# The last batch's a and b blocks, two chunks at a time: seven matmul products for eight

## The chip, the cores and the metric

The kernel runs on one core of one Trainium2 chip. The metric is the device time of one execution in microseconds (us), smaller is better. A core has TensorE (PE, matmuls; PEld is its loading of weights), VectorE (DVE), ScalarE (ACT), GpSimd (POOL) and SyncE (SP, which here issues DMAs). Each takes its own instructions in order, and they wait for each other by semaphores. SBUF is the working memory. PSUM, with eight banks of 128 x 512 floats, is where PE writes; in this kernel POOL works in SBUF only.

## The reference

The kernel computes an attention over channels and then a multiplicative feed-forward network on its output. There are 4 batches of 5824 tokens with 256 channels.

```python
qn = q / (norm(q, axis=1) + 1e-06)          # q, k, v: (4, 5824, 256)
kn = k / (norm(k, axis=1) + 1e-06)
s = kn.transpose(0, 2, 1) @ qn / tau         # 256 x 256 for each batch
a = softmax(s, axis=-1)
x = (v @ a).reshape(4 * 5824, 256)
y1 = x @ w1                                  # 256 -> 1024
y2 = x @ w2
out = (y1 * y2 @ w3) @ w_out                 # 1024 -> 1024 -> 256
```

## The kernel before

**Algebra.** w3 and w_out are multiplied once into a 1024 x 256 matrix `W_sb`. For each batch the 256 x 256 attention matrix is folded into w1 and w2, which gives `Wf`, so that the tokens v need only two products: a = v Wf1 and b = v Wf2. The output is (a * b) W_sb. Matmul inputs are bf16, sums are float32.

**Tiling.** A batch's tokens are cut into 12 chunks: 11 of 512 tokens (0 to 10) and one of 192 (11). The 1024 columns of a and b are cut into 8 blocks of 128 (index j). `emit_ab(b, c, j)` makes one block of a chunk: two matmuls for a and two for b (the 256 channels are two halves, ct), each of 512 columns (line 657). ACT casts a to bf16 (`a_sb`, line 663), and DVE multiplies it by b out of PSUM into the half-chunk tile `abh` (line 676). One such call is a slot. The a and b tiles rotate through four PSUM banks, ab0 to ab3.

**Output.** For most chunks `seven_products` computes the output as a 2 x 2 block product with seven products for eight: four sums of abh quarters, S1 to S4 (lines 589 and 592, 128 x 1024 each), then products p1 to p7, each of eight matmuls of 128 columns (line 570). ACT writes out stages of the accumulating tile A (`keep`, line 580), and DVE adds tiles B and C into the output (`join`, J, line 583), before a DMA stores the chunk. p6 reads S2, p5 reads S1, p7 reads S3 and p3 reads S4. The four S tiles have one buffer each. In batches 0 to 2 the sums are on POOL, in batch 3 on DVE. The plain way, `emit_half`, takes 32 matmuls of 256 columns (line 707) and needs no sums.

**Order.** The order of instructions is written by hand. The loop at the end runs through the slots of a batch. In each slot it emits work that is due by an estimated clock (`run_due`: loads, transposes, folds), then `emit_ab`, and then waiting output work out of the queue `pend`: entries have a slot from which they are due and a size, and a slot takes entries up to `room`, in order. So a slot of the last batch holds four matmuls of 512 columns and at most one group of eight output matmuls. The S sums are emitted out of `due_sums`.

**The next batch's weights.** During batch n - 1 the scores of batch n are computed (lines 197 to 212, over by slot 71 of 96), then the softmax, then `fold` (lines 428 to 437): eight folds of two matmuls each, evicted with a scale by ACT and DVE in turn into `Wf[n]`. Batch 3 has no next batch, so its slots hold no scores. Loads of v are issued on POOL behind a `gate`, a copy of one element that waits for the latest abh block (line 645); their transposes and the stores are issued by SP.

**Tiles.** abh, loaded pieces and some others share 21 buffers with the tag "big".

Of the kernel before, what the change touches and what calls it, by code (L numbers as in the profile page):

```python
# [9 lines left out]
AF = mybir.ActivationFunctionType  # L10
ALU = mybir.AluOpType
F32 = DT.float32
BF16 = DT.bfloat16
# [12 lines left out]
def kernel(  # L26
# [250 lines left out]
    def soft_units(n):  # L277
# [142 lines left out]
        def fold_mm(key, c2, tag="ab", on_act=True):  # L420

            w, c1, lo, hi = key
            if c2 == 0:
                turn = (lo // 512 * 4 + w * CT + c1) % 3
                home = bank(tag) if n == 0 or turn == 2 else {"tag": ("out2", "G")[turn], "bufs": 1}
                st[key] = psum.tile([P, 512], F32, name=f"fold_{n}_{w}_{c1}_{lo}", **home)
            m = st[key][:, : hi - lo]
            nc.tensor.matmul(  # L428
                m, lhsT=st["e"][:, c2, c1 * P : (c1 + 1) * P], rhs=w12[:, c2, w, lo:hi],
                start=(c2 == 0), stop=(c2 == CT - 1),  # L430
            )
            if c2 == CT - 1:
                dst = Wf[n][:, c1, w, lo:hi]
                if on_act:
                    nc.scalar.activation(out=dst, in_=m, func=AF.Copy, scale=st["rs"][:, c1 : c1 + 1])
                else:
                    nc.vector.tensor_scalar_mul(dst, m, st["rs"][:, c1 : c1 + 1])

        def fold(i, tag="ab"):
            h, rest = divmod(i, 4)  # L440
            w, c1 = divmod(rest, 2)
            for c2 in range(CT):
                fold_mm((w, c1, h * 512, (h + 1) * 512), c2, tag, i % 2 == 0 or (n == 0 and i == 7))

# [43 lines left out]
        )  # L488


    clock = [0.0]
    agenda = []

    def run_due(upto=None):
        lim = clock[0] if upto is None else upto
        while agenda and agenda[0][0] <= lim:
            _, _, cost, fn = agenda.pop(0)
            clock[0] += cost
            fn()
# [3 lines left out]
    def at(t, cost, fn):  # L503
        seq[0] += 1
        agenda.append((t, seq[0], cost, fn))
# [21 lines left out]

    def seven(b, c):
        if b == B - 1:
            return c < NCH - 2  # L530
        return (4 if b == 0 else 0) <= c < NCH - 1

    def combine_weights(step):
# [18 lines left out]
    def seven_products(b, c, k1, k2):  # L552
# [6 lines left out]
        w22 = [W_sb[:, 4 + j, P:] for j in range(4)]  # L559
        t1, t2, t3, t4 = ([T[:, i, j, :] for j in range(4)] for i in range(4))  # L560
        st, sums = {}, {}
        tags = {"A": "out0", "B": "out1", "C": "out1" if b < B - 1 else "out2"}
        adder = nc.gpsimd if b < B - 1 else nc.vector

        def product(nm, a, w, first=False):
            if first:
# [63 lines left out]
        def then(fn):  # L630
            return lambda: following.append(fn)

        if b == B - 1:
            return [S(1)], [
                [S(2), p1], [S(3), p5], [p6], [S(4), p7], [J("C", 1, 1), p2],
                [J("B", 0, 0), p4], [p3, J("C", 0, 1), store],
            ]
# [13 lines left out]
    def emit_ab(b, c, j):  # L651
        n = chunk_cols(c)
        tiles = []
        for w in range(2):
            t = psum.tile([P, 512], F32, name=f"{'ab'[w]}_{b}_{c}_{j}", **bank("ab"))
            for ct in range(CT):
                nc.tensor.matmul(  # L657
                    t[:, :n], lhsT=Wf[b][:, ct, w, j * P : (j + 1) * P], rhs=rhs_of(b, c, ct),
                    start=(ct == 0), stop=(ct == CT - 1),
                )  # L660
            tiles.append(t)
        a_sb = work.tile([P, 512], BF16, tag="a_sb", name=f"as_{b}_{c}_{j}", bufs=4)
        nc.scalar.copy(a_sb[:, :n], tiles[0][:, :n])  # L663
        if c == NCH - 1:
            if b % 2 == 0 and j == 0:
                lefts[b // 2] = work.tile([P, FT, 2, P + LEFT], BF16, tag="left", name=f"left_{b}", bufs=1)
            both = lefts[b // 2][:, j, b % 2, :]
            nc.vector.tensor_mul(both, a_sb[:, :n], tiles[1][:, :n])
            ab = both[:, :P] if b % 2 == 0 else both[:, LEFT:]
        else:  # L670
            if j == 0:
                halves[c] = [
                    in_pool.tile([P, 4, 512], BF16, tag="big", name=f"abh_{b}_{c}_{h}", bufs=BIG_BUFS) for h in range(2)
                ]
            ab = halves[c][j // 4][:, j % 4, :]
            nc.vector.tensor_mul(ab, a_sb, tiles[1])  # L676
        last_ab[0] = ab
        slot[0] += 1
        if not seven(b, c):
            if b == B - 1 or c == NCH - 1:  # L680
                lag = LAG if b == B - 1 else FT + LAG_FAST
                pend.append((slot[0] + lag, 1, lambda only=None: emit_out(b, c, j, ab, only)))
            elif j == FT - 1:
                for i in range(FT):
                    fn = lambda i=i, ab2=tuple(halves[c]): emit_half(b, c, i, ab2)
                    pend.append((slot[0] + 1 + LAG_FAST + i, 1, fn))
        elif j == FT - 1:
            sums, groups = seven_products(b, c, *halves[c])
            for i, fn in enumerate(sums):
                due_sums.append((slot[0] + 2 * i, fn))  # L690
            ready = slot[0] + 1 + (LAG_FAST if b < B - 1 else 0)
            for i, group in enumerate(groups):
                wait = 0 if b == B - 1 else i
                pend.append((ready + wait, 2, lambda group=group: [fn() for fn in group]))
        clock[0] += 4 * (n * MM_COL + MM_FIX)

    def emit_half(b, c, i, ab2):

# [212 lines left out]
    def make_agenda(b):  # L911
# [34 lines left out]
        if b == 0:  # L946
            for i in range(4):
                at(COMB + 2.6 * i, 0.0, lambda i=i: combine_weights(i))
        if n == B:
            agenda.sort()  # L950
            return
# [14 lines left out]

    for b in range(B):
        make_agenda(b)
        order = [(c, j) for c in range(NCH) for j in range(FT)]
        if b == 0:  # L970
            order[: 2 * FT] = [(c, h * 4 + j) for h in range(2) for c in range(2) for j in range(4)]
        for s, (c, j) in enumerate(order):
            run_due()
            while following:
                following.pop(0)()
            scores_due(s)
            emit_ab(b, c, j)
            lag = 0
            if b == B - 1 and c >= NCH - 2:
                lag = LAG_END if c == NCH - 1 else LAG + (LAG_END - LAG) * (j + 1) // FT  # L980
            room = 2
            while slot[0] > W_SLOT and len(pend) > lag and pend[0][0] <= slot[0] and pend[0][1] <= room:
                _, size, fn = pend.pop(0)
                fn()
                room -= size
                run_due()
            while due_sums and due_sums[0][0] <= slot[0]:
                due_sums.pop(0)[1]()
        run_due(1e9)
# [39 lines left out]
```

## Time and profile before

| | |
|---|---|
| median of 3 runs | 555.02 us (554.97 to 555.27) |
| span of the profiled execution, first to last instruction | 553.5 us |
| own time of the profiled execution | only its span is given; the median of the runs lies 1.5 us above it |
| PE, DVE, ACT, POOL busy | 542.1, 435.5, 375.8, 304.8 us |
| granted PE clock | 1.000 |
| last batch's first a matmul | at 431.81 us |

The profile shows one execution. A timeline line gives start, duration, engine, line of the kernel, operation, output and inputs, count, and in brackets the idle time before it with what ended it. A matmul's duration covers its way through the array; the next one starts well before it ends, so what one costs is the distance between starts. The same holds in smaller measure for DVE and ACT. A line by stretch gives the stretch, its length, the busy time of PE, PEld, DVE, ACT and POOL with counts in brackets, the granted clock of PE as a fraction, the share of the DMA engines and GB/s.

### The profile page before, as it was taken

How to read it: one execution, taken by the hardware profiler on the slowest of the kernel's cores; microseconds unless marked ns; L12 is line 12 of the kernel's file. 1: busy time of each engine (PE TensorE's matmuls, PEld its weight loads, DVE VectorE, ACT ScalarE, POOL GpSimd, SP SyncE). 2: the span in 40 equal slices, each digit the busy share in tenths (PEclk: the TensorE clock that was granted, in tenths of full speed). 3: DMA queues.
4: the chain of work that ended last, by engine and by line, in shares of the span. 5: the costliest groups of instructions: out<-in, count | busy, mean ns of one | idle time of the engine just before them, and what ended most of it. 6: DMA issues, size and time to landing. Idle time of an engine off the chain costs nothing.

```text
span 553.5 us, 12330 instructions
## 1 busy us (share of the span) xinstructions
PE 542.1 (98%) x4630; PEld 352.9 (64%) x4630; DVE 435.5 (79%) x789; ACT 375.8 (68%) x757; POOL 304.8 (55%) x257
## 2 busy tenths in 40 slices
PE   7799999999999999999999999999999999999997
PEld 4564577766666666666667566666666666666665
DVE  5567747899976787988876788888877688988984
ACT  5436647788866777777766777777766666566663
POOL 4150022678889678889887588898987400010000
PEclk9999999999999999999999999999999999999999
DMA  9999888975666879576554777875650245343102
GB/s 213 211 206 209 167 164 201 224 180 82 152 140 155 191 150 165 126 147 136 128 127 122 153 153 156 164 147 124 147 115 40 83 117 117 91 110 82 77 40 97
DMA packets 74972, 77.61 MB, mean 140 GB/s; under 512 B 54176, under 2 KB 58784, under 8 KB 74912
## 3 DMA queue, kind: packets, MB, share of 16 engines
q0 software_dynamic: 15616, 38.93, 40.3%
q1 hardware_dynamic: 58928, 37.17, 24.2%
q8 instruction: 36, 0.59, 0.4%
q10 hardware_dynamic: 368, 0.72, 0.3%
q14 instruction: 24, 0.20, 0.1%
HBM read 78.91 MB, written 23.86 MB: 186 GB/s over the span
## 4 chain that ended last, share of the span: by engine, by line
PE 93%; DMA 5%; DVE 0%; ACT 0%; POOL 0%; issue 0%; POOLq 0%
PE a L657 28%; PE b L657 28%; PE prodA L570 13%; PE prodC L570 6%; PE G L200 5%; PE prodB L570 3%; DMA k<-in_k_dram 3%; PE o L707 3%; PE fold L428 2%; DMA q<-in_q_dram 2%; PE o_out L738 2%; PE w L882 1%; PE G L271 0%; PE narrow L452 0%; PE sqq L259 0%
## 5 line engine op out<-in xcount | busy, mean ns | idle before, releaser
L676 DVE TENSOR_TENSOR abh<-as,b 128x512 bf16<-128x512 bf16 x352 | 240.0, 684 | 82.0 <-ACT as L663 76.2
L663 ACT CAST as<-a 128x512 bf16<-128x512 f32 (+1 forms) x384 | 215.4, 562 | 94.8 <-PE a L657 61.5
L657 PE MATMUL a<-vT,Wf 128*128 128x512 bf16 x704 | 209.4, 379 | 0.1
L657 PE MATMUL b<-vT,Wf 128*128 128x512 bf16 x704 | 209.4, 379 | 0.0
L657 PEld LDWEIGHTS <-Wf 128*128 128x128 bf16 x1536 | 141.1, 98 | 100.6 <-issue 0.8
L570 PEld LDWEIGHTS <-S 128*128 128x128 bf16 x1248 | 82.6, 98 | 34.3
L212 DVE TENSOR_TENSOR acc<-acc,sq 128x512 f32<-128x512 f32 x132 | 91.6, 694 | 3.0 <-ACT sq L197 1.9
L580 ACT COPY osb<-prodA 128x256 f32<-128x256 f32 x156 | 58.1, 372 | 42.0 <-PE prodA L570 41.4
L589 POOL TENSOR_TENSOR S<-abh,abh 128x1024 bf16<-128x1024 bf16 x29 | 61.7, 2127 | 32.1 <-DVE abh L676 16.6
L570 PEld LDWEIGHTS <-abh 128*128 128x128 bf16 x936 | 62.0, 98 | 25.7 <-issue 0.2
L592 POOL TENSOR_TENSOR S<-S,abh 128x1024 bf16<-128x1024 bf16 x29 | 61.8, 2131 | 1.9
L592 POOL TENSOR_TENSOR S<-abh 128x1024 bf16<-128x1024 bf16 x29 | 61.8, 2131 | 0.1
L592 POOL TENSOR_TENSOR S<-abh,S 128x1024 bf16<-128x1024 bf16 x29 | 61.7, 2129 | 0.1
L645 POOL COPY gate_t<-abh 1x1 bf16<-1x1 bf16 x39 | 7.2, 185 | 80.1 <-DVE abh L676 79.9
L570 PE MATMUL prodA<-comb_T,S 128*128 128x128 bf16 x624 | 47.6, 219 | 0.0
L200 PE MATMUL G<-k,q 128*128 128x256 bf16 x276 | 47.0, 273 | 0.0
L197 ACT ACTIVATE sq<-q 128x512 f32<-128x512 bf16 x69 | 43.8, 634 | 0.0
L197 ACT ACTIVATE sq<-k 128x512 f32<-128x512 bf16 x69 | 43.4, 628 | 0.0
L583 DVE TENSOR_TENSOR osb<-prodC,osb 128x256 f32<-128x256 f32 x78 | 32.5, 417 | 0.0
L200 PEld LDWEIGHTS <-q 128*128 128x128 bf16 x276 | 23.9, 98 | 3.6
L570 PE MATMUL prodB<-W_sb,abh 128*128 128x128 bf16 x312 | 23.8, 219 | 0.1
L570 PE MATMUL prodC<-comb_T,S 128*128 128x128 bf16 x312 | 23.8, 219 | 0.0
(139 smaller groups left out, 444.0 us busy)
## 6 DMA issues: line engine op xcount, KB each, us to landing
out_dram<-osb SPq DMA_DIRECT2D x44, 512.0 KB, 3.2
k<-in_k_dram POOLq DMA_DIRECT2D x19, 512.0 KB, 8.3
v<-in_v_dram POOLq DMA_DIRECT2D x19, 512.0 KB, 5.2
q<-in_q_dram POOLq DMA_DIRECT2D x18, 512.0 KB, 5.8
w_wout<-in_moe_w_dram POOLq DMA_DIRECT2D x1, 2048.0 KB, 21.6
k<-in_k_dram POOLq DMA_DIRECT2D x4, 320.0 KB, 6.5
v<-in_v_dram POOLq DMA_DIRECT2D x4, 320.0 KB, 5.4
q<-in_q_dram POOLq DMA_DIRECT2D x3, 320.0 KB, 5.2
```

What stands on the lines that cost most here:

```text
L197: nc.scalar.activation(out=sqs[0][:, :, part, :], in_=src[:, o : o + 2, :], func=AF.Square)
L200: nc.tensor.matmul(G[:, ct, :], lhsT=qt[:, i, ct * P : (ct + 1) * P], rhs=kt[:, i, :], start=(pr == 0 and part == 0 and ct == 0), stop=(pr ...
L212: nc.vector.tensor_add(accs[n], accs[n], sqs[0][:, part - 2])
L570: nc.tensor.matmul(st[nm][:, i, :], lhsT=a[:, j, i * P : (i + 1) * P], rhs=w[j], start=(first and j == 0 and i == 0), stop=(j == 3), skip_ ...
L580: nc.scalar.copy(quarter(r, d), st["A"])
L583: nc.vector.tensor_add(quarter(r, d), st[nm], quarter(r, d))
L589: adder.tensor_add(x, a21, a22)
L592: adder.tensor_sub(x, u, w)
L657: nc.tensor.matmul(t[:, :n], lhsT=Wf[b][:, ct, w, j * P : (j + 1) * P], rhs=rhs_of(b, c, ct), start=(ct == 0), stop=(ct == CT - 1),)
L663: nc.scalar.copy(a_sb[:, :n], tiles[0][:, :n])
L676: nc.vector.tensor_mul(ab, a_sb, tiles[1])
L707: nc.tensor.matmul(t[:, k, :], lhsT=ab2[j // 4][:, j % 4, (2 * h + k) * P : (2 * h + k + 1) * P], rhs=W_sb[:, j, :], start=(j == 0 and k = ...
```

## The change

In the last batch (b = 3) chunks are taken in pairs: (0, 1), (2, 3), (4, 5) and (6, 7). For every even block jw of a and b, the 2 x 2 product (a and b columns of the block, by two chunks, over the two channel halves) is computed with seven matmuls of 512 columns where there were eight; the odd block jn is computed as before. A pair has four rounds k, each of four slots (sub 0 to 3), for blocks 2k and 2k + 1 of both chunks.

- In a round PE writes X = Wf * v, which ACT copies to Y (PSUM to PSUM). T = S0 * T0 goes by ACT to `t5` in SBUF. X gets a second product, and DVE writes Z = X + t5 into T's bank; after a third product on X, DVE writes `b1` = X + t5 to SBUF; Z, Y and X each get one product more. Y is cast by ACT; products of a and b are on DVE as before. X takes ab0 and ab1 in turn, T and Z are in ab2, plain a blocks in ab3, plain b blocks in the other one of ab0 and ab1 and in G, which also holds Y.
- `token_sum`: four sums of v tiles for each pair, 128 x 512 in bf16, on POOL: for pair 0 in batch 2, for the others during the pair before, one each round.
- `weight_sums`: in the folds of batch 3, ACT evicts all eight, and DVE makes eight fused multiply-and-add operations for four sums of weights. The order of folds within a half changes.
- In chunks 0 to 6 of batch 3 the sums S1 to S4 are on POOL, and the seven products follow the order and lag of the earlier batches. Chunk 7 is computed the plain way. Chunks 8 and 9 keep their order, with the sums on DVE, but come later in the queue.
- `room` is 4 for single-chunk slots of the last batch, 2 in pairs.
- Batch 2's chunk 10 emits its products every second slot.

The diff, cut to its core:

```diff
         def fold_mm(key, c2, tag="ab", on_act=True):
...
-                turn = (lo // 512 * 4 + w * CT + c1) % 3
+                turn = (lo // 512 * 4 + ((1 - w) if n in PAIRED else w) * CT + c1) % 3
...
-                if on_act:
+                if n in PAIRED:
+                    nc.scalar.activation(out=dst, in_=m, func=AF.Copy, scale=st["rs"][:, c1 : c1 + 1])
+                    weight_sums(w, c1, lo, hi, m)
+                elif on_act:
...
+        def weight_sums(w, c1, lo, hi, m):
...
+            S = [wsums[n][x // 2][:, x % 2, lo:hi] for x in range(4)]
+            b1 = Wf[n][:, 0, 1, lo:hi]
+            todo = {
+                (1, 0): [], (1, 1): [(0, b1, ALU.add)], (0, 0): [(1, S[0], ALU.subtract), (2, b1, ALU.subtract)],
+                (0, 1): [(3, S[1], ALU.add)],
+            }
+            for x, other, op in todo[w, c1]:
+                nc.vector.scalar_tensor_tensor(
+                    out=S[x], in0=m, scalar=st["rs"][:, c1 : c1 + 1], in1=other, op0=ALU.mult, op1=op
+                )
...
+    PAIRED = {B - 1: (0, 2, 4, 6)}
...
+    def token_sum(b, c, i):
...
+        b11, b12, b21, b22 = (rhs_of(b, c + d, ct) for ct in range(CT) for d in range(2))
+        if i == 0:
+            nc.gpsimd.tensor_sub(t[:, 0], b12, b11)
+        elif i == 1:
+            nc.gpsimd.tensor_sub(t[:, 1], t[:, 0], b22)
+        elif i == 2:
+            nc.gpsimd.tensor_sub(t[:, 2], b22, b12)
+        else:
+            nc.gpsimd.tensor_add(t[:, 3], b21, t[:, 1])
...
-            return c < NCH - 2
+            return c < NCH - 2 and c != 1 + max(PAIRED[b])
...
-        adder = nc.gpsimd if b < B - 1 else nc.vector
+        adder = nc.vector if b == B - 1 and c > max(PAIRED[b]) else nc.gpsimd
...
+    def queue_products(b, c, delay=0):
+
+        if not seven(b, c):
+            return queue_halves(b, c, delay)
+        sums, groups = seven_products(b, c, *halves[c])
+        late = len(sums) == 1
+        if late:
+            pend.append((slot[0], 0, sums[0]))
+        for i, fn in enumerate(() if late else sums):
+            due_sums.append((slot[0] + delay + 2 * i, fn))
+        ready = slot[0] + delay + 1 + (0 if late else LAG_FAST)
+        for i, group in enumerate(groups):
+            step = 0 if late else 2 * i if (b, c) == (B - 2, NCH - 2) else i
+            pend.append((ready + step, 2, lambda group=group: [fn() for fn in group]))
...
+    def pair_begin(b, c, k):
...
+        st["X"] = psum.tile([P, 512], F32, name=f"X_{b}_{c}_{k}", tag=f"ab{x}", bufs=1)
+        j = slice(2 * k * P, (2 * k + 1) * P)
+        mm512(st["X"], Wf[b][:, 0, 0, j], rhs_of(b, c, 0), True)
+        st["Y"] = psum.tile([P, 512], F32, name=f"Y_{b}_{c}_{k}", tag="G", bufs=1)
+        nc.scalar.copy(st["Y"], st["X"])
...
+    def emit_pair(b, c, k, sub):
...
+        if sub == 0:
+            st["T"] = psum.tile([P, 512], F32, name=f"T_{b}_{c}_{k}", tag="ab2", bufs=1)
+            mm512(st["T"], S[0][:, js], T[:, 0], True)
+            st["t5"] = work.tile([P, 512], F32, tag="sq", name=f"t5_{b}_{c}_{k}", bufs=2)
+            nc.scalar.copy(st["t5"], st["T"])
+            a = plain(b, c, jn, 0, "ab3")
+            st["a"] = cast(a, f"as_{b}_{c}_{jn}")
+        elif sub == 1:
+            mm512(X, S[1][:, js], T[:, 1], False)
+            st["Z"] = psum.tile([P, 512], F32, name=f"Z_{b}_{c}_{k}", tag="ab2", bufs=1)
+            nc.vector.tensor_add(st["Z"], X, st["t5"])
+            t = plain(b, c, jn, 1, f"ab{1 - st['x']}")
+            nc.vector.tensor_mul(ab(0, jn), st["a"], t)
+            last_ab[0] = ab(0, jn)
+            mm512(st["Y"], W[:, 1, 0, js], rhs_of(b, c, 1), False)
+            st["a0"] = cast(st["Y"], f"as_{b}_{c}_{jw}")
+        elif sub == 2:
+            a = plain(b, c + 1, jn, 0, "ab3")
+            st["a"] = cast(a, f"as_{b}_{c + 1}_{jn}")
+            mm512(X, S[2][:, js], T[:, 2], False)
+            st["b1"] = work.tile([P, 512], BF16, tag="b_sb", name=f"bs_{b}_{c + 1}_{jw}", bufs=1)
+            nc.vector.tensor_add(st["b1"], X, st["t5"])
+            mm512(st["Z"], S[3][:, js], rhs_of(b, c + 1, 1), False)
+        else:
+            nc.vector.tensor_mul(ab(1, jw), st["b1"], st["Z"])
+            t = plain(b, c + 1, jn, 1, "G")
+            nc.vector.tensor_mul(ab(1, jn), st["a"], t)
+
+            def end():
+                mm512(X, W[:, 1, 1, js], T[:, 3], False)
+                if k < 3:
+                    pair_begin(b, c, k + 1)
+                elif c + 2 in PAIRED[b]:
+                    pair_begin(b, c + 2, 0)
+                nc.vector.tensor_mul(ab(0, jw), st["a0"], X)
+                last_ab[0] = ab(0, jw)
+                if k == 3:
+                    queue_products(b, c)
+                    queue_products(b, c + 1, FT)
...
+        if n in PAIRED:
+            for i in range(4):
+                at(100 + 3 * i, 0.0, lambda i=i: token_sum(n, 0, i))
...
+            late = emit_pair(b, c, j, *sub) if sub else emit_ab(b, c, j)
+            if sub and c + 2 in PAIRED[b] and sub[0] == 3:
+                token_sum(b, c + 2, j)
...
-            room = 2
+            room = 4 if b == B - 1 and not sub else 2
```

`plain` is two matmuls into a fresh tile, `cast` is ACT's cast to `a_sb`, and `mm512` is one matmul of 512 columns. In what follows M1 to M7 are the seven products of a round in the order of the algebra: M1 starts X, M7 is T.

## The prediction

> **What bounds the kernel now.** I read the page's busy shares and the chain that ended last, then the busy times by stretch, then the timeline of one stretch for every engine. Page:
>
> ```profile
> PE 542.1 (98%) x4630; PEld 352.9 (64%) x4630; DVE 435.5 (79%) x789; ACT 375.8 (68%) x757; POOL 304.8 (55%) x257
> ...
> PE 93%; DMA 5%; DVE 0%; ACT 0%; POOL 0%; issue 0%; POOLq 0%
> ```
>
> Busy times by stretch (length, then PE, PEld, DVE, ACT, POOL, granted clock): the start, the second half of batch 2, and two chunks of the last batch.
>
> ```profile
> 0.00:50.00 50.00, 42.71 (x332) 27.35 (x333) 29.78 (x65) 24.26 (x45) 17.56 (x33) 1.00 1.10 209
> 350.00:400.00 50.00, 50.00 (x446) 32.70 (x444) 43.39 (x78) 38.78 (x78) 44.76 (x32) 1.00 0.68 141
> 462.90:483.40 20.50, 20.50 (x188) 13.00 (x186) 17.91 (x32) 12.49 (x25) 0.70 (x2) 1.00 0.43 106
> ```
>
> PE never stops in the last batch (it starts at 431.81), DVE is 87% busy, POOL idle. A matmul less there is time won, as long as nobody makes PE wait. Timeline, starts and durations of one block:
>
> ```profile
> 440.15 0.58 ACT L663 CAST as<-a 128x512 bf16<-128x512 f32 x1 [0.39 <-PE a L657]
> ...
> 440.49 0.59 PE L657 MATMUL a<-vT,Wf 128*128 128x512 bf16 x2
> ...
> 440.77 0.69 DVE L676 TENSOR_TENSOR abh<-as,b 128x512 bf16<-128x512 bf16 x1 [0.28 <-ACT as L663]
> ...
> 440.92 0.59 PE L657 MATMUL b<-vT,Wf 128*128 128x512 bf16 x2
> ...
> 441.12 0.58 ACT L663 CAST as<-a 128x512 bf16<-128x512 f32 x1 [0.39 <-PE a L657]
> ```
>
> Two matmuls take 0.43, so 0.2155 us each. The second is issued at 440.705 and its result is read at 441.12: 0.415 from issue to reader. A cast begun at 440.15 lets DVE begin at 440.77: 0.62. Eight output matmuls (one group: 445.28 to 445.72) take 0.44. DVE and POOL in dense stretches, by their own timelines:
>
> ```profile
> 483.17 0.69 DVE L592 TENSOR_TENSOR S<-S,abh 128x1024 bf16<-128x1024 bf16 x1
> 483.77 0.68 DVE L676 TENSOR_TENSOR abh<-as,b 128x512 bf16<-128x512 bf16 x1
> 484.37 0.69 DVE L592 TENSOR_TENSOR S<-abh 128x1024 bf16<-128x1024 bf16 x1
> ```
>
> ```profile
> 402.81 0.18 POOL L645 COPY gate_t<-abh 1x1 bf16<-1x1 bf16 x1 [2.28 <-DVE abh L676]
> 403.31 0.57 POOL L120 DMA_DIRECT2D v<-in_v_dram  x1 [0.32 <-issue]
> 403.90 2.14 POOL L589 TENSOR_TENSOR S<-abh,abh 128x1024 bf16<-128x1024 bf16 x1
> 406.11 2.12 POOL L592 TENSOR_TENSOR S<-S,abh 128x1024 bf16<-128x1024 bf16 x1
> 408.19 2.12 POOL L592 TENSOR_TENSOR S<-abh 128x1024 bf16<-128x1024 bf16 x1
> 410.27 2.13 POOL L592 TENSOR_TENSOR S<-abh,S 128x1024 bf16<-128x1024 bf16 x1
> ```
>
> DVE starts an independent operation every 0.60, one that needs the last result after 0.73 (0.69 and 0.04 to start). ACT follows a 512-wide copy after 0.48 (546.42 to 546.90). POOL starts a sum every 2.08 (2.21 where it needs the one before): 8.49 a chunk; a gate with its load takes 0.9 to 1.1.
>
> **PE's work.** A round (one k: an even and an odd block for two chunks) has 15 matmuls of 512 columns for 16. Four pairs of four rounds save 16 x 0.2155 = 3.45. Chunk 7 plain costs 32 matmuls of 256 columns for 56 of 128: 8 x 0.435 (eight of line 707 take 0.87) against 7 x 0.441, +0.40. Net -3.05: 552.0, if PE never waits.
>
> **The round's chain.** Per round DVE gets two adds more (Z and b1, 128x512, PSUM and SBUF in; nearest row 694 ns) and ACT a copy more (X to Y and X's partner T to t5, less one cast). No row shows ACT copying PSUM to PSUM; bounds 0.37 (256 wide) and 0.69 (fold), I take 0.58, the same copy into SBUF. The loop: the product that reads the last plain b frees Y's bank 0.73 after its start; Y's copy, then t5's copy 0.48 later, reach DVE 0.62 after that: 1.83. Z, the next product and b1 follow at 0.60 each: b1 at 3.03; the product of b1 needs it: 3.76; the next product closes the loop at 4.36. A round can't be shorter. PE's own work is 3.23 + 0.44 per output group: 5.00 with four, 4.56 with three, and there the chain hides (laid out row by row, odd rounds wait 0.08, where a join of 0.33 comes in front). But output work is thin at first. By the emission rules pair 0 has only batch 2's chunk 10, spread over every second slot, and its small rows: rounds of 4.33, 3.67, 4.33 and 3.88 us of PE, 16.2 in all. Laid out, with joins and the wait of M7 for Z's bank, they take 4.48, 4.70, 4.75 and 4.62 = 18.55: **+2.35** (bounds: 1.2, the bare loop of 4.36 in rounds two to four, and 3.5, an estimate with each join of 0.33 in the way once a round). Pair 2's first round has none: 3.23 becomes 4.5.
>
> **POOL.** It gets the four sums of chunks 0 to 6, which frees DVE of 28 x 0.60, and four token sums a pair. No row has a 512-wide sum on POOL; between a linear fit through the gate (0.18) and the sum (2.13), 1.16, and half the spacing, 1.04, I take 1.08. A pair then needs 2 x 8.49 + 4.3 + 1.0 for a load = 22.3, PE only 19.1. From the start of pair 2: S1 waits for the last product of pair 0 (1.2); up to S3 of chunk 3 there are 15 sums (31.9), seven token sums (7.6) and two loads (2.0): 42.6. The product that reads it (p7, first round of pair 6) comes after 17.8 + 19.1 + 0.65 = 37.5 of PE's work. So PE loses **+5.1** on the way, in p6 and p7 of chunks 1 to 3, and every matmul queued behind them waits too (1.6 of it is the round's chain, which POOL's lateness otherwise would claim). Bounds: with token sums at DVE's 0.60 it is 1.7, with 1.16 it is 5.7. In the rest of pair 6 sums and piece 5's two loads keep POOL late: **+0.65** (0 to 1.5).
>
> Against this stands the Trainium skill, GPSIMD Engine Reference, section 4.1: elementwise sums belong on VectorE, GpSimd being about twice as slow. By that ratio on DVE's 0.60 a sum would be 1.2, an estimate, and POOL would never be late; this trace has 2.08 against 0.60, 3.5 times, and I go by the trace.
>
> Token sums for pair 0 come in batch 2 at 404 to 414; POOL's sums then end up to 4.3 later, and p6 of chunk 9 at 421.96 has its operand at 420.9: hidden, by 1.0. The loads queued behind sums on POOL are used 20 us later: nothing. SP's stores and transposes keep their order.
>
> **Folds** (418.5 to 426.9). ACT takes all eight evictions (4 x 0.69 more) and DVE eight fused sums (748 ns by line 437) for four: 2.1 of each 2.17 us cycle. Four ab banks cover a product that is late by one slot; 0 to 1.0, I take **+0.2**. Chunk 10's products only move.
>
> **The end.** Chunk 8's and 9's output starts late, two groups a slot. Then S1 and S2 follow chunk 7's copy and a product on DVE, and p5 and p6 stand in the next slot: by the rows waits of 0.9 at slot 84, 0.2 at 87, 0.55 at 88, **+1.6** (0 to 2).
>
> **Sum:** -3.05 + 2.35 + 5.1 + 0.65 + 0.2 + 1.6 = +6.85. The profiled execution has a span of 553.5; the median of the runs is 1.5 above, which the change does not touch: span 560.4, time 561.9.
>
> **Rivals.** (1) Faster: POOL's queue runs ahead of its readers and the chain lies behind output work, so PE stays the bound: 552.0. For it: PE waits for no one in the last batch, and POOL at 44.8 of 50 us cost nothing in batch 2. Against it: 22.3 against 19.1 a pair. It decides while all waits together stay under 3.05, that is where a POOL sum costs under 1.8 and most thin rounds hide. (2) The chain binds, POOL does not (token sums or sums cheaper than the rows): -3.05 + 2.35 + 1.6 + 0.2 + 0.2 + 1.6 = +2.9: 557.9. (3) Between: losses eat the gain, 555.0 within 0.2%. That the matmuls are not saved can be excluded by the code: 16 fewer of 512 columns.
>
> (4) The Trainium skill, TensorE: Matmul & The Clock Gate, section on psum-queue depth-cycling, says that short stops between matmul groups can make the clock fall. In 0 to 50 us PE is busy 42.7 and the granted clock stays 1.00; so I add nothing.
>
> **Chances.** The forecast 0.62, (2) 0.18, (1) 0.13, (3) 0.07. Over 0.2% (1.1 us, about what this kernel's measurement can tell from no change): faster 0.13, same 0.07, slower 0.80. The range leaves out (1) and a little above: from 555.0, where (3) lies, to 565.0, most bounds at their upper end together.
>
> **What would show it.** PE's busy share falls below 98%; PE waits on POOL S (p6, p7, line 570) between pairs 2 and 6, up to 1.2 each; waits on ACT Y and DVE Z in pair 0 and the next round; POOL busy without a gap for some 40 us, at 305 + 28 x 2.13 + 16 x 1.1 = 382; a token sum row of 1.0 to 1.2. If the token sum is under 0.7, or POOL has gaps in pair 4, the POOL term is wrong; if pair 0 takes near 16.2, the chain is.

## The result and the profile after

The changed kernel takes 563.97 us (median of four runs, 563.93 to 564.13); the kernel before took 555.00 on the same chip. The ratio is 1.0161, with an interval of 1.0146 to 1.0175: 8.97 us slower. The profiled execution took 564.13 with a span of 562.4, against 553.5 before: 8.9 more.

The page after, busy time by engine and the chain that ended last:

```profile
PE 545.0 (97%) x4583; PEld 351.1 (62%) x4590; DVE 437.2 (78%) x791; ACT 380.9 (68%) x774; POOL 380.4 (68%) x301
...
PE 84%; POOL 5%; DMA 5%; DVE 3%; ACT 1%; issue 1%; DVEq 0%; POOLq 0%; ACTq 0%
```

PE carried 93% of the chain before and carries 84% now; POOL, DVE and ACT, at 0% before, hold 9%. POOL's 380.4 us are what the sums moved to it were to cost (382). The last batch by stretches of 20 us (length, then PE, PEld, DVE, ACT, POOL, granted clock, DMA share, GB/s):

```profile
430.00:450.00 20.00, 18.87 (x141) 10.79 (x140) 15.61 (x31) 12.31 (x28) 10.00 (x9) 1.00 0.35 78
450.00:470.00 20.00, 19.05 (x138) 10.18 (x137) 17.17 (x30) 13.08 (x28) 16.51 (x11) 1.00 0.22 55
470.00:490.00 20.00, 19.52 (x172) 11.99 (x171) 17.02 (x30) 13.03 (x28) 19.90 (x14) 1.00 0.34 90
490.00:510.00 20.00, 18.91 (x163) 11.19 (x161) 16.25 (x29) 12.27 (x26) 19.82 (x14) 1.00 0.51 120
```

PE was busy for all of its stretch before; now it stops in each of these four. POOL fills 39.7 of 40 us from 470 to 510. The clock stays at 1.00 in every row, so the many short stops of PE did not touch it.

Where a start is compared with the kernel before, 0.88 us is taken off for two groups of output products that the change moves out of batch 2. Batch 3's first matmul stands at 432.80. Before it stood at 431.81, so at 430.93 without those groups: 1.87 us were lost before the first round. From there to the first product T of pair 2 (452.17) it takes 19.37 us, where PE has 16.2 of work. The stage of the folds, timeline of all engines:

```profile
420.90 1.26 ACT L435 ACTIVATE Wf<-fold,rs 128x512 bf16<-128x512 f32 x2 [0.58 <-PE fold L428]
...
421.69 0.75 DVE L455 SCALAR_TENSOR_TENSOR wsum<-fold,rs,Wf 128x512 bf16<-128x512 f32 x1 [0.65 <-ACT Wf L435]
422.55 0.75 DVE L455 SCALAR_TENSOR_TENSOR wsum<-fold,rs,wsum 128x512 bf16<-128x512 f32 x1
...
424.80 0.74 DVE L455 SCALAR_TENSOR_TENSOR wsum<-fold,rs,wsum 128x512 bf16<-128x512 f32 x1
...
428.42 0.34 DVE L708 TENSOR_TENSOR left<-as,b 128x192 bf16<-128x192 bf16 x1
428.68 0.74 DVE L455 SCALAR_TENSOR_TENSOR wsum<-fold,rs,wsum 128x512 bf16<-128x512 f32 x1
428.82 0.33 PE L697 MATMUL b<-vTt,Wf 128*128 128x192 bf16 x2 [0.92 <-DVE left L708]
```

The first sums wait for ACT (0.65): a sum needs the folded weights that ACT evicts. From 421.69 to 429.4 DVE runs almost without a gap; a product of the small chunk (`left`) stands in its queue between the sums, ends at 428.76, and the b matmul that needs its bank has waited 0.92.

One round of pair 0, timeline of PE, DVE and ACT:

```profile
437.85 0.38 PE L754 MATMUL T<-tsum,wsum 128*128 128x512 bf16 x1
...
438.49 0.57 ACT L766 COPY Y<-X 128x512 f32<-128x512 f32 x1 [1.73 <-DVE abh L824]
...
438.97 0.59 ACT L802 COPY t<-T 128x512 f32<-128x512 f32 x1
...
439.60 0.70 DVE L808 TENSOR_TENSOR Z<-X,t 128x512 f32<-128x512 f32 x1 [0.60 <-ACT t L802]
...
441.89 0.68 DVE L822 TENSOR_TENSOR abh<-bs,Z 128x512 bf16<-128x512 bf16 x1
...
442.62 0.38 PE L754 MATMUL T<-tsum,wsum 128*128 128x512 bf16 x1 [0.33 <-DVE abh L822]
```

The copy to Y takes 0.57, as taken, and the t5 copy, Z and the products follow each other as the prediction laid out. From T to T it is 4.77 us for 3.67 of PE's work.

PE's waits for POOL, timeline of PE, and POOL's own queue by its timeline:

```profile
482.89 0.62 PE L610 MATMUL prodA<-comb_T,S 128*128 128x128 bf16 x8 [0.47 <-POOL S L632]
490.95 0.62 PE L610 MATMUL prodA<-comb_T,S 128*128 128x128 bf16 x8 [0.49 <-POOL S L632]
494.12 0.62 PE L610 MATMUL prodA<-comb_T,S 128*128 128x128 bf16 x8 [0.60 <-POOL S L632]
```

```profile
490.84 1.15 POOL L526 TENSOR_TENSOR tsum<-vT 128x512 bf16<-128x512 bf16 x1
491.95 2.11 POOL L632 TENSOR_TENSOR S<-abh 128x1024 bf16<-128x1024 bf16 x1
494.04 2.11 POOL L632 TENSOR_TENSOR S<-abh,S 128x1024 bf16<-128x1024 bf16 x1
```

S3 of chunk 3 ends at 494.06, and p7, which reads it, is issued at 494.12. POOL's first sum for pair 0 began 1.22 after the start of pair 2 (1.2 was taken), and from then on POOL works without a gap until chunk 6's last sum. A token sum costs it 1.11 from start to start.

### The profile page after: what moved, and what is told of

Same layout as the page of the kernel before. It is cut to its first block, busy times and chain, and to the rows that moved or that the text cites. A ratio compares the mean times of both kernels' runs of the same rounds, so it can differ in the third digit from the quotient of the medians.

```text
span 562.4 us, 12296 instructions
## 1 busy us (share of the span) xinstructions
PE 545.0 (97%) x4583; PEld 351.1 (62%) x4590; DVE 437.2 (78%) x791; ACT 380.9 (68%) x774; POOL 380.4 (68%) x301
## 4 chain that ended last, share of the span: by engine, by line
PE 84%; POOL 5%; DMA 5%; DVE 3%; ACT 1%; issue 1%; DVEq 0%; POOLq 0%; ACTq 0%
PE a L697 23%; PE b L697 22%; PE prodA L610 11%; PE G L200 5%; PE prodC L610 5%; POOL S L632 3%; PE o L852 3%; PE prodB L610 3%; DMA k<-in_k_dram 3%; DMA q<-in_q_dram 2%; PE fold L428 2%; PE X L754 2%; PE a L754 2%; PE o_out L883 2%; PE b L754 1%; PE w L1027 1%
## 5 line engine op out<-in xcount | busy, mean ns | idle before, releaser
L716 DVE TENSOR_TENSOR abh<-as,b 128x512 bf16<-128x512 bf16 x288 | 196.2, 683 | 74.4 <-ACT as L703 69.5
L703 ACT CAST as<-a 128x512 bf16<-128x512 f32 (+1 forms) x320 | 177.8, 558 | 75.3 <-PE a L697 54.6
L697 PEld LDWEIGHTS <-Wf 128*128 128x128 bf16 x1280 | 118.5, 98 | 85.2 <-issue 2.1
L697 PE MATMUL a<-vT,Wf 128*128 128x512 bf16 x576 | 171.3, 379 | 0.2
L697 PE MATMUL b<-vT,Wf 128*128 128x512 bf16 x576 | 171.3, 379 | 0.1
L610 PEld LDWEIGHTS <-S 128*128 128x128 bf16 x1216 | 79.8, 98 | 37.1 <-POOL S L632 3.8
L629 POOL TENSOR_TENSOR S<-abh,abh 128x1024 bf16<-128x1024 bf16 x36 | 76.5, 2126 | 35.9 <-PE prodC L610 12.5
L632 POOL TENSOR_TENSOR S<-S,abh 128x1024 bf16<-128x1024 bf16 x36 | 76.6, 2127 | 2.3
L632 POOL TENSOR_TENSOR S<-abh 128x1024 bf16<-128x1024 bf16 x36 | 76.6, 2128 | 0.1
L632 POOL TENSOR_TENSOR S<-abh,S 128x1024 bf16<-128x1024 bf16 x36 | 76.6, 2126 | 0.1
L754 PEld LDWEIGHTS <-Wf 128*128 128x128 bf16 x176 | 15.8, 97 | 15.6 <-issue 4.8
```

The lines of the kernel that those rows point to most:

```text
L610: nc.tensor.matmul(st[nm][:, i, :], lhsT=a[:, j, i * P : (i + 1) * P], rhs=w[j], start=(first and j == 0 and i == 0), stop=(j == 3), skip_ ...
L629: adder.tensor_add(x, a21, a22)
L632: adder.tensor_sub(x, u, w)
L697: nc.tensor.matmul(t[:, :n], lhsT=Wf[b][:, ct, w, j * P : (j + 1) * P], rhs=rhs_of(b, c, ct), start=(ct == 0), stop=(ct == CT - 1),)
L754: nc.tensor.matmul(dst, lhsT=lhsT, rhs=rhs, start=start, stop=True, skip_group_check=True)
```

## The experiments

Each run is compared with the kernel before on the same chip; "over" means microseconds over that kernel. The changed kernel stands 8.97 over. The interval of a ratio is some 0.8 us to either side, so a difference of less than that between two runs is read from the starts in their traces and not from the medians alone.

**Chunk 8's and 9's sums earlier.** S1 to S4 are emitted in the slots before their products, no longer beside them.

```diff
-            return [S(1)], [[S(2), p1], [S(3), p5], [p6], [S(4), p7], ...
+            return [S(1), S(2), S(3), S(4)], [[p1], [p5], [p6], [p7], ...
+        steps = [4, 5, 6, 7] if c == 2 + max(PAIRED[b]) else [5, 5, 6, 7]
```

> Chunks 8 and 9's sums S1 to S4 are emitted one a slot ahead of the products (slots 75 to 78 and 84 to 86), not in the slot before their reader. Theory A (end costs 1.6 in all by these sums): 1.6 us less. Theory B (profile after: waits for S of 0.6, 0.35, 0.2 and 0.4, and 0.65 for ACT's copy of tile A, which stays): 1.2 to 1.6 us less. Rival C (the end's waits are for DVE as a whole, which has the same work): under 0.5 us less.

562.38 us, 7.26 over, ratio 1.0130 (1.0114 to 1.0145): 1.7 us won back, as theory A has it; under rival C it would be below 0.5. In the changed kernel PE's waits after 530 us are these (timeline of PE):

```profile
540.07 0.62 PE L610 MATMUL prodC<-comb_T,S 128*128 128x128 bf16 x8 [0.42 <-DVE S L629]
540.86 0.62 PE L610 MATMUL prodA<-comb_T,S 128*128 128x128 bf16 x8 [0.18 <-DVE S L632]
...
547.53 0.62 PE L610 MATMUL prodA<-comb_T,S 128*128 128x128 bf16 x8 [0.25 <-DVE S L632]
548.62 0.61 PE L610 MATMUL prodA<-comb_T,S 128*128 128x128 bf16 x8 [0.46 <-ACT osb L620]
```

With the edit only the last is left: two A products in a row, the second waiting for ACT's `keep` of the first. So the sums' waits of the prediction's last term are shown, and 0.65 of another kind stand beside them.

**Chunk 10's products not spread** over every second slot.

```diff
-            step = 0 if late else 2 * i if (b, c) == (B - 2, NCH - 2) else i
+            step = 0 if late else i
```

> Batch 2's chunk 10 emits its products every slot again, as the kernel before does: p6 and p5 come before batch 3's first round, p7, p4 and p3 in its first four slots. If the rounds' chain sets pair 0's length (4.4 us or more a round whatever PE has to do), output work inside these rounds is free, and taking 0.88 us out of them makes them no shorter: 0 to 0.9 us slower than the changed kernel (less where the work covers waits of the short slots before). Rival (PE's work sets the length there): no difference, within 0.2.

564.68 us, 9.56 over, ratio 1.0172 (1.0155 to 1.0188): 0.6 slower than the changed kernel by the medians, within what the chain allows, and inside the interval. The trace says more. The first round from T is then full (4.61 us) and pair 0's last one, with no output work left, takes 4.63 for 3.23 of PE's work. Output work that is put into a thin round is done in its waits; taken out, the round stays as long.

**Fewer token sums on POOL.** Pairs 4 and 6 read pair 2's token sums; their own eight are left out.

```diff
+        if c > 2:
+            tsums[b, c] = tsums[b, 2]
+            return
```

> Left out: the token sums of pairs 4 and 6 (eight POOL operations of 1.1 us); their products read pair 2's sums, so those outputs are wrong. DVE is given nothing. POOL's work in pairs 2 and 4 falls from 22 to 18 us a pair, below PE's 19.1, and p6 and p7 have their sums in time. Theory A (the prediction's price of POOL beyond the rounds' chain: 3.5 and 0.65): 3.5 to 4.2 us less than the changed kernel. Theory B (profile after: PE's visible waits for POOL are 1.9 and some 0.5): 1.8 to 2.6 less. Rival C (DVE or ACT is the limit there and the wait only changes its name): under 0.8 less.

561.96 us, 6.72 over, ratio 1.0120 (1.0105 to 1.0135): 2.25 us less, which is theory B. POOL's queue has gaps again before each pair's first sum (its timeline), and PE waits for no S sum of POOL from 425 us on:

```profile
472.57 2.13 POOL L632 TENSOR_TENSOR S<-abh,abh 128x1024 bf16<-128x1024 bf16 x1 [1.93 <-DVE abh L835]
...
492.21 2.13 POOL L632 TENSOR_TENSOR S<-abh,abh 128x1024 bf16<-128x1024 bf16 x1 [1.95 <-DVE abh L835]
```

From the first T of pair 2 to p7 of chunk 3 it takes 39.97 us here (451.91 to 491.88), 41.95 in the changed kernel. So of the 4.4 us over PE's work that are measured in this stretch 2.0 are POOL's own; the other 2.4 are the rounds' chain, which is there without POOL. From that p7 to pair 6's last X product it takes 18.55 us here and 18.61 in the changed kernel: in the rest of pair 6 POOL costs next to nothing.

**Token sums on VectorE** for pairs 2, 4 and 6.

```diff
+        eng = nc.gpsimd if c == min(PAIRED[b]) else nc.vector
-            nc.gpsimd.tensor_sub(t[:, 0], b12, b11)
+            eng.tensor_sub(t[:, 0], b12, b11)
...
```

> The token sums of pairs 2, 4 and 6 go from POOL to DVE; pair 0's stay on POOL. POOL then has 2 x 8.49 + 1 = 18 us of work a pair against PE's 19.1, so p6 and p7 no longer wait for it. Theory A (the prediction's prices: POOL takes what the rounds' chain doesn't take, 3.5 in pairs 2 to 4 and 0.65 in pair 6): 3.5 to 4.2 us less than the changed kernel. Theory B (the profile after: PE stands before products that read POOL's sums for some 1.9 us from 482 to 494 and 0.6 later, the rest is the chain): 1.8 to 2.6 us less. Rival C (DVE, 86% busy there, is the true limit, and whatever it is given comes back): under 1 us less, or none.

Ratio 1.0376 (1.0355 to 1.0397), some 21 us over: far outside what any theory gave. The ratio rests on two executions, 576.82 and 575.29 us; the profiled one took 590.92 at a granted clock of 0.942, and a fourth of 1463.2 us is unexplained. In the profiled one seven of the twelve token sums take 0.42 us on DVE. The other five take 1.07 to 4.01, 10.7 us more in all, and each of them ends 0.28 or 0.29 after a sum on POOL (timelines of POOL and DVE):

```profile
467.99 2.12 POOL L633 TENSOR_TENSOR S<-S,abh 128x1024 bf16<-128x1024 bf16 x1
469.32 1.07 DVE L523 TENSOR_TENSOR tsum<-vT 128x512 bf16<-128x512 bf16 x1
```

The next run shows the same at a granted clock of 0.993.

**Weight sums from SBUF.** DVE adds the folded weights that ACT wrote to SBUF, both inputs in SBUF, in place of the fused operation that reads the fold in PSUM.

```diff
-                nc.vector.scalar_tensor_tensor(
-                    out=S[x], in0=m, scalar=st["rs"][:, c1 : c1 + 1], in1=other, op0=ALU.mult, op1=op
-                )
+                nc.vector.tensor_tensor(out=S[x], in0=Wf[n][:, c1, w, lo:hi], in1=other, op=op)
```

> The eight weight sums of batch 3's folds read the folded weights back from SBUF as bf16 instead of PSUM and the scale, so DVE should take less for each than 748 ns and the fold's bank is free after ACT. The sums are of rounded weights. Theory A (folds cost 0.2): 0.2 us less. Theory B (profile after: batch 3's first matmul comes 1.9 us later than the moved products allow, after DVE's backlog in the folds): 1.2 to 1.9 us less. Rival C (ACT's eight evictions of 0.69 set the pace, not DVE): under 0.5 us less.

572.19 us, 17.1 over, ratio 1.0309 (1.0294 to 1.0325): 8.1 us slower than the changed kernel, where all three theories gave a gain. Timeline of POOL and DVE:

```profile
423.91 2.30 POOL L630 TENSOR_TENSOR S<-abh,S 128x1024 bf16<-128x1024 bf16 x1
424.34 2.15 DVE L455 TENSOR_TENSOR wsum<-Wf,wsum 128x512 bf16<-128x512 bf16 x1
426.42 0.41 DVE L455 TENSOR_TENSOR wsum<-Wf 128x512 bf16<-128x512 bf16 x1
427.68 0.41 DVE L455 TENSOR_TENSOR wsum<-Wf,wsum 128x512 bf16<-128x512 bf16 x1
428.83 2.12 POOL L627 TENSOR_TENSOR S<-abh,abh 128x1024 bf16<-128x1024 bf16 x1 [2.62 <-DVE abh L714]
429.01 2.22 DVE L455 TENSOR_TENSOR wsum<-Wf 128x512 bf16<-128x512 bf16 x1 [0.32 <-ACT Wf L435]
```

The same operation takes 0.41 while POOL is idle (426.2 to 428.8) and 2.15 and 2.22 while POOL runs a sum. Begun 0.43 and 0.18 after POOL's, it ends 0.28 after POOL's end (426.49 against 426.21, 431.23 against 430.95). So by these rows it is not over before POOL's instruction is. DVE's queue stands with it, and PE behind that:

```profile
436.06 0.48 PE L695 MATMUL b<-vTt,Wf 128*128 128x192 bf16 x2 [5.67 <-DVE left L706]
436.33 1.06 PE L608 MATMUL prodA<-comb_T,abh 128*128 128x128 bf16 x8
437.19 0.53 PE L695 MATMUL a<-vTt,Wf 128*128 128x192 bf16 x2
```

After that stop PE itself is slow: a group of eight output matmuls takes 0.86 from start to start (0.44 elsewhere) until 440.1, and the granted clock of 430 to 440 is 0.66. Some 1.8 of the 8.1 us are this pace, an estimate from the starts, and not the waits themselves. The shorter stop before it, 2.03 at 427.21, left the clock at 1.00 in 420 to 430.

The Trainium skill, SBUF — State Buffer, "Who interferes with whom", states this: a VectorE instruction with two SBUF inputs and a GpSimd instruction that reads SBUF exclude each other for a whole instruction, and one with at most one SBUF input, outside the two-port modes, does not contend. Both halves agree with this case: the fused form, whose second tensor is in PSUM, keeps its 0.74 to 0.75 in the changed kernel while POOL runs sums from 420.97 to 425.17 and from 426.28 on.

**The second half's weight sums on POOL**, emitted at the start of batch 3.

```diff
+            if lo == 512:
+                for x, other, op in todo[w, c1]:
+                    later.append((S[x], Wf[n][:, c1, w, lo:hi], other, op))
+                return
...
+            for i in range(4):
+                at(0.5 + 0.5 * i, 0.0, lambda i=i: later_sum(i))
```

> The four weight sums of the second half of the folds are made by POOL out of SBUF, at the start of batch 3, where POOL is idle until the first sums of chunk 0; first needed by pair 0's third round. DVE has four fused operations of 0.75 us less between 424 and 429. Theory: DVE's backlog there makes batch 3 start 1.9 us late, so 1.0 to 1.9 us less than the changed kernel. Rival: ACT's eight evictions and the fold's banks set the pace: under 0.4 us less.

563.04 us, 7.80 over, ratio 1.0138 (1.0123 to 1.0154): 1.17 us less, as the theory has it. Batch 3's first matmul comes at 431.6, and PE's wait of 0.92 for `left` is gone.

**No weight sums.**

```diff
-                    weight_sums(w, c1, lo, hi, m)
...
-        S = [wsums[b][h][:, x, :] for h in range(2) for x in range(2)]
+        S = [W[:, ct, w, :] for w in range(2) for ct in range(2)]
```

> Leaves out the eight operations on VectorE that form the weight sums; the pairs read the folded weights themselves in their place. Theory A (these operations are the whole loss of 1.9 us in the fold slots): batch 3's first matmul comes 1.6 to 2.0 us earlier and the kernel stands 7.0 to 7.4 us over the one before. Theory B (ScalarE's taking all eight evictions costs a part of it too): 1.0 to 1.5 us earlier, 7.5 to 8.0 us over the one before.

562.74 us, 7.63 over, ratio 1.0137 (1.0122 to 1.0152): 1.34 us less by the medians, which is theory B. Batch 3's first matmul stands at 431.06, 1.74 earlier, but all starts of an execution can be shifted together: here those ahead of the folds are 0.23 early as well. Taken from the last matmul of the softmax's sums (line 405; 417.12 in the changed kernel), batch 3's first matmul comes after 15.68 us in the changed kernel and after 15.66 to 15.68 in five other runs that leave this stage as it is. Here it comes after 14.17, and in the kernel before after 14.73, or 13.85 without the two groups. So of the 1.83 us that this stage loses by this measure (1.87 by the starts as they stand) the eight operations on DVE are 1.50. The other 0.3 has no run of its own; ACT's four more evictions, as theory B has it, and the new order of the folds are both in it.

**Pairs 2, 4 and 6 alone**; chunks 0 and 1 as before, the token sums for pair 2 at the start of batch 3.

```diff
-    PAIRED = {B - 1: (0, 2, 4, 6)}
+    PAIRED = {B - 1: (2, 4, 6)}
```

> Pairs are (2, 3), (4, 5) and (6, 7) only; chunks 0 and 1 are single, with 16 matmuls a round's worth again (+0.86 us of PE). Pair 2's token sums are made by POOL at the start of batch 3. Theory (rounds with little output work are set by their own chain, 4.4 to 5.05 us for 3.2 to 4.3 of PE: pair 0's four and pair 2's first lose some 4.5): the slots of chunks 0 and 1 run at PE's pace, pair 2 has chunk 0's output work from its first slot, POOL starts chunk 0's sums eight slots earlier, so 3.5 to 5.5 us less than the changed kernel. Rival (the waits belong to all rounds alike, a quarter of them to each pair): +0.86 - 1.5, 0.6 less or so.

562.08 us, 6.84 over, ratio 1.0120 (1.0105 to 1.0135): 2.1 us less, between the two theories. The thin rounds are fewer but not gone (timeline of PE):

```profile
467.25 0.38 PE L754 MATMUL T<-tsum,wsum 128*128 128x512 bf16 x1
468.51 0.38 PE L754 MATMUL X<-tsum,wsum 128*128 128x512 bf16 x1 [0.45 <-ACT Y L766]
471.88 0.38 PE L754 MATMUL T<-tsum,wsum 128*128 128x512 bf16 x1 [0.20 <-DVE abh L822]
473.14 0.39 PE L754 MATMUL X<-tsum,wsum 128*128 128x512 bf16 x1 [0.45 <-ACT Y L766]
476.54 0.38 PE L754 MATMUL T<-tsum,wsum 128*128 128x512 bf16 x1 [0.21 <-DVE abh L822]
```

Pair 2's last round and pair 4's first take 4.63 and 4.66 for 3.23 of work. Chunks 0 and 1 hand over their products eight slots apart and these are used up by then; a pair hands over its own only when all its rounds are done. The hole has moved.

**Y by a matmul of its own** in the five thin rounds (pair 0's four, pair 2's first), not by ACT's copy of X: one matmul more a round.

```diff
+        if c == 0 or (c, k) == (2, 0):
+            return
...
+            if "Y" not in st:
+                st["Y"] = psum.tile([P, 512], F32, name=f"Y_{b}_{c}_{k}", tag="G", bufs=1)
+                mm512(st["Y"], W[:, 0, 0, js], rhs_of(b, c, 0), True)
```

> In the five rounds with little output work (pair 0's four and pair 2's first) Y is not copied from X by ACT but made by a matmul of its own, so these rounds have 16 matmuls and no gain, and neither X's second product nor Y waits for the round before. Theory (the loop last product - bank of Y - Y's copy - t5 - Z sets their 4.6 to 5.05 us): without it DVE's six operations and the joins remain, 3.7 to 4.0, or PE's work, 3.9 to 4.6; 2.0 to 3.3 us less than the changed kernel, part of pair 2's share going to POOL. Rival (DVE as a whole sets these rounds, copy or not): within 0.5 either way.

564.58 us, 9.34 over, ratio 1.0164 (1.0147 to 1.0181). From the first T to pair 2's it takes 18.65 us, against 18.64 in the changed kernel, with 0.86 of work more. Taking the copy out won as much as the matmul cost, and no more. The theory falls; the rival's number holds, though DVE has idle time in these rounds, so its reason is not shown. The copy to Y is not the only thing that holds these rounds.

**In those rounds X's second product and Z's add right behind T**, ahead of plain a and the output group.

```diff
+        def second():
+            mm512(X, S[1][:, js], T[:, 1], False)
+            st["Z"] = psum.tile([P, 512], F32, name=f"Z_{b}_{c}_{k}", tag="ab2", bufs=1)
+            nc.vector.tensor_add(st["Z"], X, st["t5"])
...
+            if thin:
+                second()
             a = plain(b, c, jn, 0, "ab3")
```

> As the run that forms Y by a matmul of its own in the five thin rounds (no copy on ScalarE, one matmul of 0.2155 more in each), and in those rounds X's second product and Z's add stand right behind T, ahead of plain a and of the output group. PE's own work of a round is 4.05 + 0.22 = 4.27 us. Theory (two equal loops, the one left over going through T, Z, b1 and the bank of T and Z, with plain a and the output group in it): rounds of pair 0 go from 4.7-4.8 us to 4.3-4.5, pair 0 with its start from 19.4 to 17.3-18.2 us, and the kernel stands 6.8 to 7.8 us over the one before (the changed kernel: 9.0). Rival (the rounds are limited by VectorE's own chain of operations, whose order is not changed): rounds within 0.1 us of 4.75, kernel 8.7 to 9.7 us over the one before.

564.59 us, 9.48 over, ratio 1.0170 (1.0155 to 1.0185). The rounds stay at 4.55, 4.68, 4.75 and 4.66 us: the theory falls, and its loop is not the one that binds here. The rival's numbers hold. What follows T now (timeline of PE and DVE):

```profile
440.47 0.38 PE L754 MATMUL X<-tsum,wsum 128*128 128x512 bf16 x1
...
440.88 0.69 DVE L832 TENSOR_TENSOR bs<-X,t 128x512 bf16<-128x512 f32 x1 [0.32 <-PE X L754]
...
441.49 0.41 DVE L623 TENSOR_TENSOR osb<-prodC,osb 128x256 f32<-128x256 f32 x1
...
441.82 0.68 DVE L835 TENSOR_TENSOR abh<-bs,Z 128x512 bf16<-128x512 bf16 x1
...
442.55 0.38 PE L754 MATMUL T<-tsum,wsum 128*128 128x512 bf16 x1 [0.33 <-DVE abh L835]
```

But DVE too waits for PE here (0.32), so its queue alone is not the limit. PE works from T (437.87) without a gap and reaches X's third product only at 440.47; b1, a join and the product follow, then the next T.

**X's third product early too**, with b1, Z's last matmul and their product, ahead of Y and the second plain a.

```diff
+            if c == 0 or (c, k) == (2, 0):
+                third()
+                nc.vector.tensor_mul(ab(1, jw), st["b1"], st["Z"])
             nc.vector.tensor_mul(ab(0, jn), st["a"], t)
```

> As the run before it with Y by its own matmul and X's second product early; in the five thin rounds, X's third product, b1, Z's last matmul and their product now also stand earlier: behind plain b, ahead of Y, of the second plain a and of the first product on VectorE. Theory (the loop that is left is TensorE's own order: from T it works 2.6 us without a gap to X's third product, then b1, one join and the product on VectorE, then the next T, 4.7 us in all, of which Y and the second plain a are 0.87): rounds of pair 0 go to 4.1-4.4 us (VectorE's six operations and a join, 0.60 apart, are 3.9), pair 0 loses 1.3 to 2.4 us and the kernel stands 7.0 to 8.3 us over the one before. Rival (VectorE's queue sets the round whatever TensorE's order): 4.6-4.75 us, 9.0 to 9.7 us over the one before.

564.28 us, 9.17 over, ratio 1.0164 (1.0147 to 1.0181). From the first T (433.60) to pair 2's (452.08) it takes 18.48, 0.16 less than in the changed kernel. The rival's numbers hold, its reason is not borne out: DVE waits 1.9 us for X's products on PE in this stretch, and in the five rounds PE's named waits are for ACT's casts of Y (0.5) and for Z (0.2), for a product of DVE only ahead of the first T (0.36 for `left`). A new wait stands in the way (timeline):

```profile
441.02 0.59 ACT L779 CAST as<-Y 128x512 bf16<-128x512 f32 x1 [0.92 <-PE Y L754]
...
441.66 0.59 PE L754 MATMUL b<-vT,Wf 128*128 128x512 bf16 x2 [0.24 <-ACT as L779]
```

Plain b takes Y's bank, and Y now stands so late that b waits for its cast.

**Three edits together**, nothing left out: chunk 8's and 9's sums early, the second half's weight sums on POOL, pairs 2, 4 and 6 alone.

> Three edits together, all of the computation kept: chunk 8's and 9's sums early, the second half's weight sums on GpSimd, pairs 2, 4 and 6 alone (their first token sums in batch 3's first slots). One by one they took 1.7, 1.2 and 2.1 us off the changed kernel. If they act in different stages they add up: 5.0 us off, 3.6 to 4.4 us over the kernel before. If the second and third share what they take away (both move the beginning of GpSimd's row of work, and the added sums stand ahead of the token sums in its queue): 3.5 to 4.3 us off, 4.7 to 5.5 over. No theory expects it faster than the kernel before: each pair takes 0.86 us of matmuls off, and the full rounds wait 0.1 to 0.2 us each, the thin ones 0.7.

559.55 us, 4.44 over, ratio 1.0078 (1.0061 to 1.0095). One by one the edits took 1.7, 1.2 and 2.1 off; together 4.5. That is 0.04 above the range of "they add up" and nearer to it than to the rival. POOL has slack now (its timeline), and PE's waits for it are gone:

```profile
465.48 1.14 POOL L539 TENSOR_TENSOR tsum<-vT,tsum 128x512 bf16<-128x512 bf16 x1
472.03 2.12 POOL L640 TENSOR_TENSOR S<-abh,abh 128x1024 bf16<-128x1024 bf16 x1 [5.40 <-DVE abh L844]
```

This is the best version with pairs, and it is still slower than the kernel before. Its twelve rounds save 12 x 0.2155 = 2.59 us and chunk 7 costs 0.40. Two thin rounds (4.63 and 4.68 us for 3.23 of work) lose 2.85 at once. A round with three output groups takes 4.66 for 4.55 of work, one with four 5.18 for 5.00: even behind full cover 0.11 to 0.18 of the 0.2155 saved is waited away.

## Why the prediction was right or wrong

The forecast was 561.9 us, slower; measured 563.97. The direction and the main mechanisms hold, the sum was 2.1 us short. By its terms, measured from the starts in the trace:

| term | forecast | measured |
|---|---|---|
| folds and the slots after them | +0.2 | +1.87 |
| pair 0's four rounds | +2.35 | +3.15 |
| pair 2's start to p7 of chunk 3 | +5.1 | +4.4 |
| rest of pair 6 | +0.65 | +0.6 |
| end | +1.6 | +2.2 |
| matmuls saved, chunk 7 plain | -3.05 | -3.05, by count |
| sum | +6.85 | +9.2 (span: +8.9) |

**Folds: the step that failed.** The term took DVE's work per fold as 2.1 of a 2.17 us cycle and let four banks cover a late product, bounds 0 to 1.0. It left out that a weight sum cannot start before ACT's eviction (the 0.65 above), which puts DVE a slot behind, and that the short slots of the small chunk come right after, where a block's PE work is too short to hide a 0.75 operation between two products. Taking half of these sums off DVE won 1.17, all of them 1.34 by the medians and 1.50 within the stage. The upper bound of 1.0 was too low as well: it went with the 2.17 us cycle of the full slots.

**Pair 0.** Rounds two to four were laid out at 4.70, 4.75 and 4.62 and measured 4.77, 4.83 and 4.72; the excess of 0.1 each is small. The first, from batch 3's first matmul, took 5.05 for 4.48: its T also waits 0.36 for DVE's last `left` product, which the layout did not have. The prediction named one loop, through Y's bank. The runs show that this loop alone does not set the rounds: without Y's copy, and with the products reordered twice, pair 0 still takes 18.5 to 18.65 from T to T. That several loops of about the same length lie there fits this, but is not shown. Which single order would bring a thin round down to PE's 3.7 to 4.3 was not found and stays open.

**POOL.** Forecast 42.6 us from pair 2's start to p7 of chunk 3, measured 41.95 against 37.5 of PE's work. What was off is the split: 1.6 was given to the rounds' chain and 3.5 to POOL. By the run with half of the token sums, POOL's own is 2.0; the chain holds the other 2.4: 1.4 in pair 2's first round, the rest in the full rounds, where 0.08 had been laid out for every second one and 0.1 to 0.2 is measured in all. The token sum was taken at 1.08 and costs 1.11. The PE waits for POOL at 482.89, 490.95 and 494.12 decide for the trace's 3.5 to one in the price of a sum, under which POOL falls behind its readers. The Trainium skill's ratio of about two (GPSIMD Engine Reference, 4.1) would, by the prediction's estimate of 1.2 us a sum, have kept it ahead of them. In the rest of pair 6 the term of 0.65 meets the measured 0.6 by luck: it was put down to POOL's lateness, and the run with half of the token sums, where PE waits for no sum of POOL, has the same length there within 0.06. By that it is the chain again.

**End.** The forecast waits of 0.9, 0.2 and 0.55 are found at 540.07 with 540.86, at 546.34 and at 547.53, together about 1.6; moving the sums won 1.7. The p7 that waits 0.65 behind ACT's `keep` was not foreseen.

**Rivals.** Rival 1 (552.0) is excluded: PE stops in every stretch from 430 to 510. Rival 2 (the chain alone, 557.9) is excluded by POOL's 2.0 and by the folds. The clock of the changed kernel stayed at 1.00, so nothing had to be added for it. The steps taken at nothing held: of PE's 1.6 us of visible waits for POOL on the whole page all lie between 482 and 495, so the token sums in batch 2 were hidden.

## What to carry to other kernels

A trick that saves one matmul in sixteen must be paid out of the 0.2155 us it saves: here even a round full of other work gave back 0.11 to 0.18 of it in bank and chain waits, so ask what a round's dependence chain leaves before counting what the algebra takes off. Price the one-time preparation in the slots where it is emitted: the shortest slots, not the mean ones, decide whether a queue that is 97% full makes the next engine wait. Before moving an elementwise sum between VectorE and GpSimd, look at what the other is running and at how many inputs lie in SBUF.

## What the runs showed of the hardware that was not expected

A VectorE addition with both inputs in SBUF, 0.41 us alone, took 1.69 to 2.33 us when POOL was running a 128 x 1024 sum, and ended about 0.3 us after it; eight such operations in place of fused ones that read PSUM made the kernel 8.1 us slower, some 1.8 of it by a lower clock after a stop of PE of 5.67 us. Moving twelve token sums from POOL to VectorE cost some 12 us, where POOL's being late had cost about 2. In the kernel before, the sums of the last batch were on VectorE with both inputs in SBUF at 0.69 us: POOL was busy 0.70 of 20.5 us there. The row that priced a sum on VectorE was taken beside an idle POOL.
